# Column maxima of k by 32x32 transposes and a trip through DRAM, and another order of the first loads, in a fused linear-attention and expert kernel

## The chip, the cores and the metric

The kernel runs on one core of a Trainium2 chip. The metric is the device time of one execution in microseconds (us), the median of several runs. Before the change it is 898.88 us, the median of 3 runs (898.53 to 898.95).

## The reference

The first half is linear attention over 8 batches, 8 heads, 576 positions and 64 channels: q is normalised by a softmax over its channels, k by a softmax over its positions, and no score matrix is formed. The second half is a two-layer network over the 4608 tokens with an activation between its layers.

```python
q_s = np.exp(q - np.max(q, axis=-1, keepdims=True))
q_s = q_s / (np.sum(q_s, axis=-1, keepdims=True) + 1e-09)
k_s = np.exp(k - np.max(k, axis=2, keepdims=True))      # over the 576 positions
k_s = k_s / (np.sum(k_s, axis=2, keepdims=True) + 1e-09)
kv = np.einsum('bhsd,bhse->bhde', k_s, v)
x = np.einsum('bhsd,bhde->bhse', q_s, kv)               # tokens x 512
h = x @ w_in                                            # 512 x 2048
g = h * np.clip(h + 3.0, 0.0, 6.0) / 6.0
return (g @ w_out).astype(np.float32)                   # 2048 x 512
```

What the change touches is the maximum of each of k's columns over the 576 positions.

## The kernel before, in words

Two heads are worked on together (a "head pair" `hp`, four of them to a batch, called a head below), so that 2 x 64 channels fill the 128 partitions. Tokens go in nine blocks `j` of 512. The float32 products run as three products of a high and a low part each (`split`, L121). The weights come as float64 pairs of words (`load_w`, L126, 1 MB for each of 16 slices `f`) and are decoded to float32 high and low parts by ScalarE and VectorE (`decode`, L134).

Blocks 0 and 1 use plain products (`gemm1`, L557, and `gemm2`, L574); beside block 1, sums of weights are formed and written to DRAM (`fast_weights`, L446). Blocks 2 to 8 use `fast_pair` (L493): seven smaller products in place of eight for a pair of slices, whose weights are fetched from DRAM by `fetch` (L481) into a ring of twelve places, one new fetch after each product. `fill` (L656) puts the second layer's products of the pair before between them. `steps` (L627) hands out the attention of the next block in small steps, two to a pair.

Attention for one head is `attention` (L305). In batches 0 and 1 ("early") k arrives transposed, channels on partitions; its maxima lie one to a partition, where the exponential can use them as a bias, and TensorE flips the result. From batch 2 on k arrives twice: transposed (`kt`, one buffer) for the maximum alone, and straight (`ke`, two buffers), positions on partitions, in which form it is used. There the maximum is needed as a row, the same on all partitions. VectorE reduces `kt` to `km` (L333); GpSimd spreads it over 128 columns in `kb` (L335, one buffer); TensorE flips `kb` into `pm` in PSUM (L347, through `flip`, L96, so that its trace line is L97); VectorE subtracts `pm` from `ke` (L348) and ScalarE takes the exponential (L351). `kv_of` (L201) then forms the product with v (`pkv`), and `px` (from L374 on) multiplies it with q.

The order of instructions on each engine is fixed when the program is built, by a scheduler that works through a simulated time: whichever instruction is ready first goes first, and among those that are ready the one that stands earlier in the program. From block 1 on TensorE's instructions stay in program order (`ordered`, L85). Nearly all transfers are issued by SP, whose queue is in order too: an issue that waits holds those behind it. At the start ScalarE's queue issues the four loads of q for batch 0 (L193).

The start (L604 to L613): for each of four heads `load_first` issues kT on SP and q on ScalarE's queue; the first half of weight slice 0 goes after head 1; then the four v, the second half of slice 0, and slices 1 to 5.

Of the kernel before, what the change touches and what calls it, by code (L numbers as in the profile page):

```python
# [10 lines left out]
F32 = mybir.dt.float32  # L11
F32R = mybir.dt.float32r
U32 = mybir.dt.uint32
AF = mybir.ActivationFunctionType
# [4 lines left out]
P = 128  # L19
TB = 512  # L20
QD = 32
# [9 lines left out]
def attention_moe(  # L31
# [27 lines left out]
    nc = tc.nc  # L59

    B, NP, _, S = kT.shape
# [6 lines left out]
    NCH = S // P + 1  # L68
# [5 lines left out]
    att = ctx.enter_context(tc.tile_pool(name="att", bufs=1))  # L74
    xp = ctx.enter_context(tc.tile_pool(name="xp", bufs=2))
    moe = ctx.enter_context(tc.tile_pool(name="moe", bufs=2))
    dr = ctx.enter_context(tc.tile_pool(name="dr", bufs=1, space=bass.MemoryType.DRAM))
    ps_a = ctx.enter_context(tc.tile_pool(name="ps_a", bufs=2, space=PSUM))
# [6 lines left out]
    def ordered(ins):  # L85
        if in_order:
            tc.keep_in_program_order(ins)
# [8 lines left out]
    def flip(out, in_):  # L96
        ordered(nc.tensor.transpose(out, in_, ident))  # L97
# [7 lines left out]
    three = const.tile([P, 1], F32, name="three")  # L105
# [5 lines left out]
    def place(f, dt, name):  # L111
        return wp.tile([P, 4 * DM], dt, name=name, tag=f"w{f}")
# [13 lines left out]
    def load_w(f, sides=(0, 1)):  # L126
        if f not in raws:
            raws[f] = place(f, U32, f"raw{f}")
        a, b = 2 * DM * sides[0], 2 * DM * (sides[-1] + 1)
        nc.sync.dma_start(  # L130
            raws[f][:, a:b], w[f].rearrange("p s n -> p (s n)")[:, a:b]
        )
# [56 lines left out]
    def load_first(hp):  # L189
        t = borrow(f"kq{hp}")  # L190
        kt, qt, qT = t[:, 0:S], cut(t, S, NC4, 2, D), t[:, S + TB : S + 2 * TB]
        nc.sync.dma_start(kt, kT[0, hp])
        nc.scalar.dma_start(qt, q[0, hp])  # L193
        t = borrow(f"kv{hp}")
        vt, ke = cut(t, 0, NCH, 2, D + 1), cut(t, NCH * 2 * (D + 1), NCH, P)
        first[hp] = kt, qt, qT, vt, ke

    def load_first_v(hp):
        nc.sync.dma_start(first[hp][3], v[0, hp])
# [60 lines left out]
    def k_softmax(j, km, ke, kt):  # L260

        nc.vector.tensor_reduce(km, kt, axis=AX.X, op=ALU.max, negate=True)
        nc.scalar.activation(kt, kt, AF.Exp, bias=km)
        yield
        pool, tag = (ps_a, "pa") if j else (ps_o, "po")
        pe = pool.tile([P, TB], F32, name="pe", tag=tag)
        pe2 = pool.tile([P, TB], F32, name="pe2", tag=tag)
        for c in range(NC4):
            flip(pe[:, c * P : (c + 1) * P], kt[:, c * P : (c + 1) * P])
        flip(pe2[0:TAIL, 0:P], kt[:, TB:S])  # L270
        nc.scalar.copy(ke[:, 0:NC4].rearrange("p c n -> p (c n)"), pe)
        nc.scalar.copy(ke[0:TAIL, NC4], pe2[0:TAIL, 0:P])
# [32 lines left out]
    def attention(j, hp):  # L305
# [5 lines left out]
        if not j:  # L311
            kt, qt, qT, vt, ke = first[hp]
        else:
            if j < B:
                kt = att.tile([P, S], F32, name="kt", bufs=1)
                nc.sync.dma_start(kt, kT[j, hp])
                ke = att.tile([P, NCH, P], F32, name="ke", bufs=2)
# [9 lines left out]
        if j < B:  # L327
            km = att.tile([P, 1], F32, name="km", bufs=2)
            if early:
                ks = k_softmax(j, km, ke, kt)  # L330
                next(ks)
            else:
                nc.vector.tensor_reduce(km, kt, axis=AX.X, op=ALU.max)  # L333
                kb = att.tile([P, P], F32, name="kb", bufs=1)
                nc.gpsimd.tensor_copy(kb, km.broadcast_to([P, P]))  # L335
        if early:
            q_softmax(qt, j == 1, nc.vector if j else nc.gpsimd)
        else:
# [3 lines left out]
        if early:  # L342
            next(ks, None)
        elif j < B:

            pm = ps_a.tile([P, TB], F32, name="pm", tag="pa")
            flip(pm[:, 0:P], kb)  # L347
            nc.vector.tensor_sub(  # L348
                ke, ke, pm[:, 0:P].rearrange("p (o n) -> p o n", o=1).broadcast_to([P, NCH, P])
            )  # L350
            nc.scalar.activation(ke, ke, AF.Exp)  # L351
        if early:
            pool, tag = (ps_a, "pa") if j else (ps_o, "po")
# [19 lines left out]
        pool, tag = (ps_a, "pa") if j else (ps_h, "ph")  # L373
# [217 lines left out]
    def store(j, po):  # L591
        for t in range(NTT):
# [8 lines left out]
                    nc.scalar.mul(ob, po[t], 1.0 / 6.0)  # L601
            nc.sync.dma_start(out[j * TB + t * P : j * TB + (t + 1) * P, :], ob)

    for hp in range(NP):  # L604
        load_first(hp)
        if hp == 1:
            load_w(0, (0,))
    for hp in range(NP):
        load_first_v(hp)
    load_w(0, (1,))  # L610
    AHEAD = 6
    for f in range(1, AHEAD):
        load_w(f)  # L613
    units = [attention(0, hp) for hp in range(NP)]
    for unit in units:
        next(unit)
# [10 lines left out]
    def steps():  # L627
        for j in range(1, NB):
            heads = range(NP) if j < FAST else (0, 2, 1, 3)
            for hp in heads:  # L630
                unit = attention(j, hp)
                for step in range(4):
                    next(unit, None)
                    if j == FAST and step == 3 and hp != 3:
                        continue
                    yield
                next(unit, None)
# [121 lines left out]
```

## Time and profile before

| what | before |
|---|---|
| median of 3 runs | 898.88 us |
| the profiled execution | 901.36 us |
| its span, first to last instruction | 899.0 us |
| TensorE busy (matmul) | 862.0 us, 96% |
| VectorE busy | 624.6 us, 69% |
| ScalarE busy | 459.1 us, 51% |
| GpSimd busy | 149.0 us, 17% |
| granted TensorE clock, mean | 0.992 |
| moved by DMA | 182.04 MB |

Engines are named PE (TensorE's matmuls), PEld (its weight loads), DVE (VectorE), ACT (ScalarE), POOL (GpSimd) and SP. Matmuls are pipelined, so that the durations of single ones overlap: what one costs is read from the distance between starts. The shares of busy time are means over stretches that differ, so they are read stretch by stretch.

### The profile page before, as it was taken

What the parts mean: (1) busy time and instruction counts of PE and PEld (TensorE: products, weight loads), DVE (VectorE), ACT (ScalarE), POOL (GpSimd) and SP (SyncE); (2) the same over time, 40 slices, a digit from 0 to 9 for tenths busy, and PEclk for the clock granted to TensorE, in tenths of its full rate; (3) what the DMA queues carried; (4) which work ended last, traced back from release to release, by engine and by line L of the source; (5) the groups of instructions that cost most, each with busy time, mean ns of one, the idle gap of its engine ahead of it and who ended that gap; (6) DMA issues with size and microseconds to landing.
All of it is one profiled execution on the core that took longest, in us unless ns stands there. A gap on an engine that the chain in (4) does not pass through costs nothing.

```text
span 899.0 us, 15285 instructions
## 1 busy us (share of the span) xinstructions
PE 862.0 (96%) x5380; PEld 737.0 (82%) x5380; DVE 624.6 (69%) x1265; ACT 459.1 (51%) x937; POOL 149.0 (17%) x329
## 2 busy tenths in 40 slices
PE   5799979999989999999999999999999999999998
PEld 3567656878778888888888888888888888988896
DVE  6999998889767666676776676767676655444333
ACT  6998634445445445545545554445554544443333
POOL 4021432130302121112121211112121200100000
PEclk9999999999999999999999999999999999999999
DMA  9983432538568667766776677776755565557541
GB/s 362 415 330 110 126 105 71 172 106 286 171 210 267 210 213 235 234 213 209 230 239 213 211 223 249 217 216 189 245 170 165 166 220 174 172 174 224 170 141 47
DMA packets 96986, 182.04 MB, mean 202 GB/s; under 512 B 9744, under 2 KB 24080, under 8 KB 94992
## 3 DMA queue, kind: packets, MB, share of 16 engines
q1 hardware_dynamic: 96336, 180.03, 62.0%
q10 hardware_dynamic: 576, 1.05, 0.4%
q8 instruction: 43, 0.70, 0.3%
q14 instruction: 31, 0.25, 0.1%
HBM read 156.93 MB, written 24.12 MB: 201 GB/s over the span
## 4 chain that ended last, share of the span: by engine, by line
PE 72%; DVE 7%; DMA 4%; ACT 2%; issue 1%; POOL 0%; SPq 0%; DVEq 0%; ACTq 0%; POOLq 0%
PE po L91 35%; PE ph L91 28%; PE pz L91 4%; DMA qt<-in_qf_dram 2%; PE pkv L91 2%; PE px L91 2%; DVE qT_lo L124 1%; DMA out_dram<-ob 1%; DVE w L124 1%; DVE m L302 1%; ACT qT_hi L123 1%; DVE x_hi L124 1%; DVE ob L599 1%; DVE x_lo L124 0%; DMA wf<-w 0%
## 5 line engine op out<-in xcount | busy, mean ns | idle before, releaser
L91 PE MATMUL po<-w,w 128*128 128x512 f32 x1008 | 261.5, 394 | 1.3 <-DVE ob L599 0.9
L91 PEld LDWEIGHTS po<-w,w 128*128 128x128 f32 x1008 | 178.4, 189 | 31.9 <-DVE ob L599 2.3
L91 PE MATMUL ph<-x_lo,w 128*128 128x256 f32 (+1 forms) x800 | 152.0, 304 | 1.1 <-ACT second L529 0.8
L91 PEld LDWEIGHTS ph<-w,w 128*128 128x128 f32 x1008 | 133.5, 190 | 13.9 <-DVE second L530 4.9
L91 PE MATMUL ph<-w,w 128*128 128x256 f32 x1008 | 140.6, 284 | 3.0 <-DVE second L530 3.0
L91 PE MATMUL ph<-x_hi,w 128*128 128x256 f32 (+1 forms) x592 | 138.3, 338 | 4.7 <-ACT w L123 3.4
L91 PEld LDWEIGHTS ph<-x_lo,w 128*128 128x128 f32 x800 | 116.6, 189 | 15.8 <-ACT second L529 1.2
L123 ACT CAST w<-g 128x512 fp32r<-128x512 f32 x112 | 69.5, 620 | 86.4 <-DVE g L536 43.5
L91 PEld LDWEIGHTS ph<-x_hi,w 128*128 128x128 f32 x592 | 93.4, 192 | 19.5 <-ACT w L123 5.5
L124 DVE TENSOR_TENSOR w<-g,w 128x512 fp32r<-128x512 f32 x112 | 77.1, 689 | 39.6 <-ACT w L123 39.5
L91 PE MATMUL po<-w 128*128 128x512 f32 x336 | 86.8, 394 | 0.1
L91 PE MATMUL po<-w,g_hi 128*128 128x512 f32 x256 | 70.1, 413 | 3.3 <-ACT g_hi L123 3.3
L124 DVE TENSOR_TENSOR qT_lo<-m,qT_hi 128x512 fp32r<-128x512 f32 x28 | 25.9, 925 | 66.4 <-ACT qT_hi L123 66.3
L91 PEld LDWEIGHTS po<-w 128*128 128x128 f32 x336 | 59.4, 188 | 10.8 <-ACT w L123 0.5
L91 PEld LDWEIGHTS po<-w,g_hi 128*128 128x128 f32 x256 | 48.1, 194 | 15.8 <-ACT g_hi L123 5.5
L284 POOL COPY swap<-qm 32x16 f32<-32x16 f32 x112 | 35.3, 316 | 125.0 <-DVE qm L292 120.9
L551 ACT ACTIVATE g<-second,three 128x512 f32<-128x512 f32 x56 | 40.5, 723 | 29.8 <-DVE second L549 27.3
L535 ACT ACTIVATE g<-ph,three 128x256 f32<-128x256 f32 x56 | 26.5, 473 | 56.0 <-PE ph L91 55.6
L552 DVE SCALAR_TENSOR_TENSOR g<-g,second 128x512 f32<-128x512 f32 x56 | 38.9, 695 | 19.8 <-ACT g L551 19.8
L91 PE MATMUL pz<-x_hi,w 128*128 128x256 f32 x336 | 49.4, 283 | 0.0
L530 DVE TENSOR_TENSOR second<-second,ph 128x256 f32<-128x256 f32 x56 | 23.0, 410 | 36.7 <-ACT second L529 36.6
L536 DVE SCALAR_TENSOR_TENSOR g<-g,ph 128x256 f32<-128x256 f32 x56 | 23.2, 414 | 31.5 <-ACT g L535 31.5
(121 smaller groups left out, 1265.5 us busy)
## 6 DMA issues: line engine op xcount, KB each, us to landing
w<-wf SPq DMA_DIRECT2D x392, 256.0 KB, 3.1
raw<-in_w_dram SPq DMA_DIRECT2D x15, 1024.0 KB, 14.5
out_dram<-ob SPq DMA_DIRECT2D x36, 256.0 KB, 3.2
vt<-in_v_dram SPq DMA_DIRECT2D x28, 325.0 KB, 3.5
wf<-w SPq DMA_DIRECT2D x16, 512.0 KB, 4.2
kt<-in_kT_dram SPq DMA_DIRECT2D x28, 288.0 KB, 2.9
ke<-in_k_dram SPq DMA_DIRECT2D x24, 320.0 KB, 2.9
qt<-in_qf_dram SPq DMA_DIRECT2D x28, 256.0 KB, 3.1
```

The lines of the kernel that those rows point to most:

```text
L91: nc.tensor.matmul(out, lhsT, rhs, start=start, stop=stop, skip_group_check=goes_on)
L123: nc.scalar.copy(hi, src)
L124: engine.tensor_sub(lo, src, hi.bitcast(F32))
L284: nc.gpsimd.tensor_copy(swap[r : r + QD], stat[o : o + QD])
L302: nc.vector.transpose(qT, qt)
L530: nc.vector.tensor_add(second[:, HT:], second[:, HT:], y)
L535: nc.scalar.activation(r[:, HT:], x, AF.Relu, bias=three, scale=1.0)
L536: nc.vector.scalar_tensor_tensor(r[:, HT:], r[:, HT:], 6.0, x, op0=ALU.min, op1=ALU.mult)
L551: nc.scalar.activation(r, second, AF.Relu, bias=three, scale=1.0)
L552: nc.vector.scalar_tensor_tensor(r, r, 6.0, second, op0=ALU.min, op1=ALU.mult)
L599: nc.vector.tensor_scalar_mul(ob, po[t], 1.0 / 6.0)
```

## The change

From batch 2 on the maximum takes another way. GpSimd spreads `km` over 32 columns only (`kx[:, 0]`); VectorE transposes the four 32x32 blocks of it (`kx[:, 1]`), after which the first partition of each block holds 32 maxima as a row; SP stores those four rows (512 bytes in all) to DRAM (`kd`, two buffers) and loads them again into all 128 partitions (`kb`, 64 KB). VectorE subtracts `kb`, which is now in SBUF. TensorE's flip and its place in PSUM go.

At the start, an exponential of one column (`three`) is put ahead of everything, after which `three` is written anew by GpSimd. Slice 0 of the weights is loaded whole after head 1, the v of heads 0 and 1 go behind kT of heads 2 and 3, and the v of heads 2 and 3 follow.

```diff
             else:
                 nc.vector.tensor_reduce(km, kt, axis=AX.X, op=ALU.max)
+                kx = att.tile([P, 2, QD], F32, name="kx", bufs=1)
+                nc.gpsimd.tensor_copy(kx[:, 0], km.broadcast_to([P, QD]))
+                nc.vector.transpose(kx[:, 1], kx[:, 0])
+                kd = dr.tile([P], F32, name="kd", bufs=2)
+                nc.sync.dma_start(kd.rearrange("(r n) -> r n", n=QD), kx[0:P:QD, 1])
                 kb = att.tile([P, P], F32, name="kb", bufs=1)
-                nc.gpsimd.tensor_copy(kb, km.broadcast_to([P, P]))
+                nc.sync.dma_start(
+                    kb, kd.rearrange("(o n) -> o n", o=1).broadcast_to([P, P])
+                )
...
         elif j < B:
-            pm = ps_a.tile([P, TB], F32, name="pm", tag="pa")
-            flip(pm[:, 0:P], kb)
             nc.vector.tensor_sub(
-                ke, ke, pm[:, 0:P].rearrange("p (o n) -> p o n", o=1).broadcast_to([P, NCH, P])
+                ke, ke, kb.rearrange("p (o n) -> p o n", o=1).broadcast_to([P, NCH, P])
             )
             nc.scalar.activation(ke, ke, AF.Exp)
...
+    nc.scalar.activation(three, three, AF.Exp)
+    nc.gpsimd.memset(three, 3.0)
     for hp in range(NP):
         load_first(hp)
         if hp == 1:
-            load_w(0, (0,))
-    for hp in range(NP):
+            load_w(0)
+        if hp > 1:
+            load_first_v(hp - 2)
+    for hp in (2, 3):
         load_first_v(hp)
-    load_w(0, (1,))
```

## Rows read from the trace of the kernel before

**Rows 1.** The profile's page: the busy time of each engine with its share of the span, and what the transfers moved in 40 equal slices of the span.

```profile
PE 862.0 (96%) x5380; PEld 737.0 (82%) x5380; DVE 624.6 (69%) x1265; ACT 459.1 (51%) x937; POOL 149.0 (17%) x329
...
GB/s 362 415 330 110 126 105 71 172 106 286 171 210 267 210 213 235 234 213 209 230 239 213 211 223 249 217 216 189 245 170 165 166 220 174 172 174 224 170 141 47
```

**Rows 2.** Busy time by stretches. Columns: the stretch and its length in us, the busy time of each engine in it with the number of instructions, the granted TensorE clock, the share of the DMA engines' time, GB/s.

```profile
30.00:142.00 112.00, 99.83 (x472) 74.30 (x472) 108.26 (x152) 78.98 (x158) 26.30 (x23) 0.96 0.54 195
142.00:250.00 108.00, 107.17 (x549) 85.47 (x548) 92.44 (x196) 50.55 (x92) 26.15 (x62) 1.00 0.52 168
...
300.00:700.00 400.00, 397.85 (x2728) 351.94 (x2727) 274.74 (x611) 199.02 (x426) 67.46 (x185) 1.00 0.69 216
```

**Rows 3.** The waits of TensorE from 28 to 142 us: what waited for whom, us in all, times, the longest.

```profile
PE px L91 <- DVE kv L213: 7.3, 3, 3.9
```

**Rows 4.** The waits of TensorE from 142 us to the end, the longest group.

```profile
PE ph L91 <- DVE second L530: 3.0, 5, 1.8
```

**Rows 5.** TensorE in order of time from 368 to 390 us: start, us, then engine, line, operation, what it writes and reads, and how many.

```profile
384.40 0.27 PE L97 MATMUL pm<-ident,kb 128*128 128x128 f32 x1
...
385.23 1.75 PE L91 MATMUL po<-w,w 128*128 128x512 f32 x7
386.81 0.88 PE L91 MATMUL ph<-x_lo,w 128*128 128x256 f32 x6
387.53 1.55 PE L91 MATMUL po<-w,w 128*128 128x512 f32 x6
```

**Rows 6.** The waits of VectorE from 4 to 32 us.

```profile
DVE m L146 <- ACT m L145: 2.3, 2, 2.0
DVE qr L255 <- POOL kq L258: 0.8, 1, 0.8
DVE qr L255 <- ACT kq L254: 0.8, 1, 0.8
```

**Rows 7.** SP's queue in order of time from 0 to 9 us: when the two halves of the first weights are issued.

```profile
1.65 0.43 SPq L130 DMA_DIRECT2D raw<-in_w_dram  x1
...
8.45 0.44 SPq L130 DMA_DIRECT2D raw<-in_w_dram  x1
```

**Rows 8.** The transfers issued from 0 to 8 us, and those issued at 8.4 to 8.5 us: times, KB each, us from issue to landing (first half, second half).

```profile
raw<-in_w_dram SPq DMA_DIRECT2D x1, 512.0 KB, 6.4
...
raw<-in_w_dram SPq DMA_DIRECT2D x1, 512.0 KB, 6.6
```

**Rows 9.** ScalarE in order of time from 3 to 17 us. In brackets: how long it was idle before, and what ended that.

```profile
4.53 1.28 ACT L263 ACT_TABLE_LOAD   x1 [4.53 <-DMA kq<-in_kT_dram]
5.82 1.47 ACT L263 ACTIVATE kq<-kq,km 128x576 f32<-128x576 f32 x2
...
16.18 1.15 ACT L145 ACTIVATE m<-raw 128x1024 f32<-128x1024 f32 x1
```

**Rows 10.** All engines in order of time from 0 us: ScalarE's queue issuing the four q loads, and GpSimd writing `three`.

```profile
0.74 1.85 ACTq L193 DMA_DIRECT2D kq<-in_q_dram  x4
...
1.02 0.10 POOL L106 MEMSET three<- 128x1 f32 x1
```

**Rows 11.** Groups of instructions by line and shape, over the whole span: busy us, mean ns of one, then the idle time before them.

```profile
L302 DVE STREAM_TRANSPOSE m<-qt 128x512 f32<-128x512 f32 x28 | 19.6, 700 | 0.0
...
L300 DVE TENSOR_TENSOR qt<-qt,qr 128x512 f32<-128x512 f32 x28 | 19.3, 688 | 0.7
...
L285 DVE TENSOR_TENSOR qm<-qm,swap 128x16 f32<-128x16 f32 x28 | 4.8, 170 | 8.1 <-POOL swap L284 8.1
```

**Rows 12.** The instructions on the tile `pm`: duration in ns (least, median, most), start of the first and of the last in us, shapes.

```profile
L97 PE MATMUL pm<-ident,kb x24: 270/271/272, 158.8 to 687.9; 128*128 128x128 f32 x24
L348 DVE TENSOR_TENSOR ke<-ke,pm x24: 801/809/823, 159.1 to 688.3; 128x640 f32<-128x640 f32 x24
```

**Rows 13.** The same view of the tile `ke`: its loads.

```profile
L319 SPq DMA_DIRECT2D ke<-in_k_dram x24: 328/333/497, 96.0 to 646.6; - x24
```

**Rows 14.** VectorE in order of time from 110.5 to 161.5 us: the maxima of k, the first, third and fourth of 24 (the second lies between the first two).

```profile
110.61 0.75 DVE L333 TENSOR_REDUCE km<-kt 128x1 f32<-128x576 f32 x1
...
121.09 0.74 DVE L333 TENSOR_REDUCE km<-kt 128x1 f32<-128x576 f32 x1
...
160.77 0.74 DVE L333 TENSOR_REDUCE km<-kt 128x1 f32<-128x576 f32 x1
```

**Rows 15.** The view of the tensor `out_dram`: its 36 stores of 256 KB, from issue to landing.

```profile
DMA to landing us min/median/max: 2.0/3.2/4.6
```

**Rows 16.** TensorE in order of time from 368 to 390 us: the first products of two successive pairs.

```profile
367.77 0.88 PE L91 MATMUL pz<-x_hi,w 128*128 128x256 f32 x6
...
378.98 0.87 PE L91 MATMUL pz<-x_hi,w 128*128 128x256 f32 x6
```

**Rows 17.** All engines in order of time from 236 to 264 us: one of VectorE's scalings of the output.

```profile
258.85 0.69 DVE L599 TENSOR_SCALAR ob<-po 128x512 f32<-128x512 f32 x1 [3.74 <-DMA out_dram<-ob]
```

**Rows 18.** The same view: TensorE's two waits around it.

```profile
258.10 0.97 PE L91 MATMUL ph<-x_lo,w 128*128 128x256 f32 x6 [0.83 <-ACT second L529]
...
260.86 0.98 PE L91 MATMUL ph<-w,w 128*128 128x256 f32 x6 [1.79 <-DVE second L530]
```

**Rows 19.** Busy time by stretches again, columns as in rows 2: the granted clock after that wait.

```profile
261.80:265.10 3.30, 3.30 (x16) 3.11 (x15) 3.30 (x8) 1.93 (x4) 0.00 (x0) 0.50 0.61 190
```

**Rows 20.** The waits from 250 us to the end: VectorE for the loads of q.

```profile
DVE qm L292 <- DMA qt<-in_qf_dram: 16.0, 16, 2.2
```

## The prediction, made before the changed kernel was run

> **What bounds the kernel now.** I began with the share of each engine: TensorE is busy for 96% of the span [rows 1], so the time is TensorE's work plus its gaps, and the question is where the gaps lie and who makes them. The table by stretches answers it [rows 2]. From 30 to 142 us VectorE is busy for 108.26 of 112 us and TensorE for only 99.83: VectorE, which still decodes the weights, sets the pace. From 142 to 250 us TensorE is busy for 107.17 of 108, from 300 to 700 us for 397.85 of 400: there the pace is TensorE's, and VectorE (275 of 400) has room. TensorE's waits agree: from 28 to 142 us the longest, 7.3 us, are for VectorE's kv [rows 3]; from 142 us to the end its longest group is 3.0 us [rows 4]. So three rules. An instruction taken from TensorE after 142 us is gained whole. A microsecond that VectorE gains or loses before 142 us moves all that follows by about one. VectorE's work after 142 us is free while it has room.
>
> **Part 1: the flips leave TensorE.** Of 24 heads (batches 2 to 7, four each) one 128x128 transpose goes. Its own duration, 0.27 us, is not its price, since matmuls overlap. From the start of the transpose at 384.40 to the next po group at 385.23 are 0.83 us; the same six products without it take 0.72 us (386.81 to 387.53) [rows 5]. So one costs 0.11 us, and 24 cost 2.6 us, all after 142 us: **-2.6 us**. Bounds: 0, if TensorE then waits where it worked before, and 24 x 0.27 = -6.5. The wait that goes with the flip (for kb) shows on TensorE nowhere in [rows 3, 4], so nothing more is won there.
>
> **Part 2: the order at the start.** VectorE has three stops between its first load and 32 us that another order could fill: 2.3 us for the decode's first operation, 0.8 us for GpSimd's product and 0.8 us for an exponential [rows 6], 3.9 us together. The long one is a load: the second half of the first weights is issued at 8.45 us [rows 7] and needs 6.6 us [rows 8], so it is there at about 15.1, and ScalarE begins to decode at 16.18 [rows 9]. In the new order both halves go as one transfer of 1 MB third in SP's queue; the first half was issued at 1.65 and needed 6.4 us, so it was there at 8.1. The transfers run at 415 GB/s once they are under way (second of the 40 slices [rows 1]), so 512 KB take 1.3 us and the whole is there at about 9.4. What pays is what is moved behind it: head 2's keys come 1.3 us later, head 3's keys 1.3 + 0.8 (behind one v of 325 KB) = 2.1 us later, the v of heads 1 to 3 about 1.3 us later; ScalarE's queue for q shares the same engines and its third and fourth load come about 1.3 us later. While VectorE waits for those, it has the decode's five operations at hand, if the schedule puts it there. I take the two stops of 2.0 and 0.8 us after 12.9 us as filled and give 0.8 back for the later heads: **-2.0 us**, between -3.9 (all stops filled) and +1.9.
>
> The +1.9 comes from the new exponential of one column. Today the table load of 1.28 us starts at 4.53, when the first keys are there, and the first exponential at 5.82 [rows 9]. Hiding it is worth 1.3 us on ScalarE and can shorten only the stop for the exponential, which the 3.9 us hold already; I count it at zero. But the new instruction needs `three`, written at 1.02 to 1.12 us, and ScalarE's queue also issues the four q loads from 0.74 us on [rows 10]. If it stands ahead of them, the first q is issued at 1.12 + 1.28 + 0.2 = 2.6 instead of 0.74 us: 1.9 us late, and q's maxima with it. I think it stands behind at least the first load, as that needs nothing. The memset that restores `three` waits for ScalarE on GpSimd's queue, whose next work, head 0's subtraction, needs q's maxima first: nothing. The Trainium skill (ScalarE: Activation LUTs, What ACT_TABLE_LOAD costs) adds a drain of about 1.4 us to the load's 1.28; by it this step would give up to 2.7 us. The trace disagrees: the exponential begins 1.29 us after the load does, with no drain between them [rows 9].
>
> **Part 3: what VectorE gets.** 24 transposes of 128x32. The nearest rows are 0.70 us for 128x512 and 0.17 us for a 128x16 operation [rows 11]; I take 0.2 us, as at 32 columns the fixed part rules (ends 0.15 and 0.70). The subtraction now reads SBUF twice; 128x512 with both operands there takes 0.69 us [rows 11], so 128x640 takes 0.86 against 0.81 now [rows 12]. After 142 us that is 21 x 0.25 = 5 us in VectorE's idle 31%: zero, and at most 5 us were that room gone. GpSimd's copy becomes smaller, on an engine that waits most of the time: zero.
>
> Before 142 us it counts. Three of the maxima already run there, the first at 110.61 and the last at 121.09 us; the fourth only at 160.77 [rows 14], because kb is held until the first flip, in TensorE's order, at 158.8 [rows 12]. That brake goes. The subtractions no longer wait for TensorE: k has two buffers and is loaded from 96.0 us on [rows 13], while the first subtraction comes at 159.1 [rows 12]. And kx, kd and kb together can hold more maxima. So work from after 142 us, where it was free, can be pulled to where VectorE is full. The least is three transposes, 0.6 us; the most two subtractions (1.6), three more maxima (2.2) and their transposes (1.0), 4.8 us. The other way, the three maxima could fall behind 142 us: -2.2. I take the three transposes and one subtraction: **+1.4 us**.
>
> **Part 4: the trip through DRAM.** Per head SP gets a store of 512 bytes, which waits for the transpose, and a load of 64 KB, which waits for the store and for the subtraction of the head before. Landing takes 2.0 us in the quickest store of the trace and 3.2 in the middle [rows 15], so the trip takes 4 to 6.4 us. Between two heads lie (687.9 - 158.8) / 23 = 23.0 us [rows 12]: it is covered, **0 us**. Behind these two on SP stand the weight loads, the stores and the loads of q, k and v. The weights come twelve products ahead, at seven products in 11.2 us (from one pz group to the next [rows 16]), that is 19 us less 2 to 5 for landing: SP may stand for some 14 us before TensorE starves. The bytes are 1.6 MB more on 182. The Trainium skill speaks against such a step (DMA: Bandwidth & Descriptors, Anatomy of one DMA): about 2.0 us per transfer whatever its size, so about 4 us for the pair, which for 24 heads would add 96 us if nothing lay beside it. The rows agree on the 2 us and show the cover of 23.
>
> **Sum.** -2.6 - 2.0 + 1.4 + 0 = -3.2 us. The profiled execution took 901.36 us (span 899.0), so it would take 898.2; its distance to the median of the runs, 898.88, is 2.5 us, which I keep: **895.7 us**, 0.35% faster.
>
> **Rivals.** *The start gives nothing back.* The later heads, or q behind the table load, hold VectorE as long as the decode did (part 2 between -1 and +1.9), or more maxima are pulled forward. For it: attention's last head, not the decode, ended the wait before the first products (TensorE's longest wait there is for VectorE's kv [rows 3]). Against it: 2 us of that stop are plainly the load's. With part 2 at zero and part 3 at +2.2: 898.5 us. That is also the time if the steps do nothing that counts, the flip's 2.6 us apart.
>
> *Slower: VectorE stuck behind a transfer at a pair's sixth or seventh product.* VectorE works in order; its subtraction now waits for a transfer (kb, or k itself, which so far had landed long before the flip), and SP's longer queue delays stores and q loads. The price is seen once: at 258.85 us VectorE had waited 3.74 us for a store of the output, TensorE then 0.83 and 1.79 us [rows 17, 18], and its granted clock fell to 0.50 (1.2 GHz) from 261.8 to 265.1 us [rows 19], 1.7 us more: 4.3 us. Against it: 16 waits for q, 16.0 us together [rows 20], cost TensorE almost nothing, so a wait decides only from about 3.5 us on. Two more such places give -3.2 + 8.6: 904.3 us.
>
> *Faster than the sum:* the stop at 258.85 goes, because four subtractions have left the stretch before it: -3.2 - 4.3, 891.4 us.
>
> **Chances.** Forecast 0.50, nothing from the start 0.20, slower 0.18, faster than the sum 0.12. A change of 0.2%, 1.8 us, is about what can be told from none here. Of the forecast's cases 0.06 fall within it, with part 3 near its upper end; of the first rival 0.16 do, and 0.02 on either side; of the slower one 0.02, a single short stop. So faster 0.44 + 0.02 + 0.12 = 0.58, same 0.24, slower 0.02 + 0.16 = 0.18. For 8 in 10 the range runs from 891.5 (all stops at the start filled and nothing pulled forward give 892.4, and the fastest case lies below) to 900.5 (the start lost at +1.9 and 2.3 pulled forward); beyond it lie the slower rival's price and half of the fastest.
>
> **What would show it.** Right: no pm rows; a po group 0.71 us after a six-product group at each of those places; the first decode near 10 us and no stop of 2 us on VectorE between 13 and 18; the table load over before 4.5 us; L333 and the subtraction waiting for no transfer. Wrong: q loads issued after 2.5 us; five or more maxima, or subtractions, before 142 us with TensorE's waits there above the present ones; VectorE's subtraction behind a transfer for over 3.5 us with a wait of TensorE right after it.

## The result and the profile after

The changed kernel took 908.37 us (median of 4 runs, 906.72 to 910.28) against 898.91 for the kernel before (898.53 to 899.58): ratio 1.0095, 95% interval 1.0078 to 1.0112. It is slower by about 9.5 us, where 895.7 was forecast. The profiled execution took 910.28 us, span 908.3, 9 us more than the one before (901.36, 899.0).

TensorE's busy time moved by 1.2 us [rows 1], so 8 of the 9 us are gaps:

```profile
PE 863.2 (95%) x5356; PEld 738.8 (81%) x5356; DVE 631.3 (70%) x1289; ACT 455.9 (50%) x938; POOL 149.7 (16%) x330
```

To find the gaps I divided both traces at the same places in the work: at block 1's first product, at the first product of the first `fast_pair` (block 2), and at the last product. The table by stretches, columns as in [rows 2], first of before, then of after:

```profile
0.00:149.84 149.84, 122.80 (x628) 90.99 (x629) 136.89 (x205) 103.60 (x194) 39.86 (x46) 0.97 0.60 224
149.84:249.97 100.13, 99.30 (x514) 79.11 (x513) 85.20 (x187) 48.22 (x88) 21.91 (x57) 1.00 0.54 175
249.97:894.90 644.93, 639.53 (x4240) 566.88 (x4238) 401.88 (x874) 306.97 (x655) 87.19 (x226) 1.00 0.65 201
```

```profile
0.00:143.60 143.60, 120.83 (x628) 91.24 (x629) 136.91 (x204) 104.85 (x197) 40.79 (x49) 0.95 0.63 235
143.60:260.90 117.30, 104.64 (x509) 82.11 (x508) 101.32 (x232) 46.77 (x87) 27.21 (x73) 0.96 0.59 191
260.90:903.84 642.94, 637.28 (x4220) 565.47 (x4219) 392.35 (x854) 303.95 (x654) 81.66 (x208) 1.00 0.63 197
```

Up to block 1 after is 6.2 us ahead, blocks 2 to 8 give 2.0 more, and block 1 alone loses 17.2: 100.1 us became 117.3, with 16 us more of VectorE in it. What VectorE does there that it did later before, or not at all, in after and then in before (groups by line and shape, columns as in [rows 11]):

```profile
L333 DVE TENSOR_REDUCE km<-kt 128x1 f32<-128x576 f32 x20 | 14.8, 739 | 2.4 <-DMA kt<-in_kT_dram 2.2
...
L337 DVE STREAM_TRANSPOSE kx<-kx 128x32 f32<-128x32 f32 x21 | 4.2, 202 | 2.0 <-POOL kx L336 1.7
```

```profile
L333 DVE TENSOR_REDUCE km<-kt 128x1 f32<-128x576 f32 x5 | 3.7, 742 | 0.0
```

The tiles of after say how far these ran ahead (columns as in [rows 12 to 14]):

```profile
L333 DVE TENSOR_REDUCE km<-kt x24: 702/742/754, 124.7 to 238.5; 128x1 f32<-128x576 f32 x24
...
L339 SPq DMA_DIRECT2D kd<-kx x24: 499/500/1139, 127.0 to 245.2; - x24
L341 SPq DMA_DIRECT2D kb<-kd x24: 319/320/955, 128.6 to 636.9; - x24
L354 DVE TENSOR_TENSOR ke<-ke,kb x24: 805/824/827, 133.4 to 659.5; 128x640 f32<-128x640 f32 x24
```

All 24 maxima, transposes and stores lie between 124.7 and 245.2 us; the loads of `kb` and the subtractions that use them come as late as 636.9 and 659.5. Before, the maxima were spread out as the subtractions were: eight of them by the first fast pair, where after has all 24. The two buffers of `kd` held nothing: the stores were up to 16 heads ahead of the loads. If `kd` has only two places in DRAM, most of these rows were overwritten before they were loaded. Whether they were is not shown, and the result hardly tells: a softmax over the positions does not depend on what was subtracted from its column, but for overflow and the 1e-09.

How TensorE felt it, its waits in block 1 in after and then in before:

```profile
PE px L91 <- DVE kv_lo L124: 4.8, 4, 1.5
PE px L91 <- ACT kv_hi L123: 4.6, 3, 2.3
PE po L91 <- ACT g_hi L123: 2.4, 2, 2.0
PE po L91 <- DVE g_lo L124: 0.8, 1, 0.8
```

```profile
PE po L91 <- ACT g_hi L123: 0.6, 1, 0.6
PE po L91 <- DVE g_lo L124: 0.2, 1, 0.2
```

12.6 us of waits against 0.8. The other 5.3 us are in TensorE's busy time (104.64 against 99.30) and are mostly clock: in after three stretches of 3.4 us at 0.50 (1.2 GHz) stand in block 1, in before none. That is about half their length, 1.7 us for each, and each begins at most 1.0 us after one of these waits ended (product started at 148.54 after 1.97 us, at 193.40 after 1.51, at 237.30 after 2.32):

```profile
149.50:152.90 3.40, 2.84 (x7) 2.29 (x8) 3.33 (x9) 1.14 (x2) 1.11 (x4) 0.50 0.31 91
193.90:197.30 3.40, 3.40 (x9) 2.67 (x8) 3.40 (x5) 2.93 (x7) 2.70 (x3) 0.50 0.16 33
238.30:241.70 3.40, 3.11 (x8) 2.55 (x9) 2.06 (x5) 2.88 (x7) 1.72 (x3) 0.50 0.99 359
```

So block 1 is 99.3 us of products, plus waits, plus clock; the same sum, with 98 to 100 us of products, holds for every kernel below.

One head (the third of block 1) shows how a wait arises: VectorE in after, in order of time, from the first `rk` to `kv_lo`, then ScalarE, then TensorE:

```profile
209.06 0.14 DVE L210 TENSOR_SCALAR rk<-pkv 128x1 f32<-128x1 f32 x1
209.13 0.73 DVE L333 TENSOR_REDUCE km<-kt 128x1 f32<-128x576 f32 x1
...
210.63 0.83 DVE L354 TENSOR_TENSOR ke<-ke,kb 128x640 f32<-128x640 f32 x1
211.37 0.15 DVE L211 RECIPROCAL rk<-rk 128x1 f32<-128x1 f32 x1
...
212.37 0.34 DVE L213 SCALAR_TENSOR_TENSOR kv<-pkv,rk,mask 128x128 f32<-128x128 f32 x1
...
215.99 0.21 DVE L337 STREAM_TRANSPOSE kx<-kx 128x32 f32<-128x32 f32 x1
216.13 0.25 DVE L124 TENSOR_TENSOR kv_lo<-kv,kv_hi 128x128 fp32r<-128x128 f32 x1
```

```profile
213.28 0.69 ACT L573 ACTIVATE g<-ph,three 128x512 f32<-128x512 f32 x1 [1.00 <-PE ph L91]
213.87 0.61 ACT L123 CAST w<-ob 128x512 fp32r<-128x512 f32 x1
214.38 0.30 ACT L123 CAST kv_hi<-kv 128x128 fp32r<-128x128 f32 x1
```

```profile
206.47 0.95 PE L91 MATMUL pkv<-vt,ke 128*64 128x65 f32 x20
...
214.73 0.44 PE L91 MATMUL px<-qT_hi,kv_hi 128*128 128x384 f32 x1 [1.26 <-ACT kv_hi L123]
...
216.43 0.45 PE L91 MATMUL px<-qT_hi,kv_lo 128*128 128x384 f32 x1 [1.09 <-DVE kv_lo L124]
```

From `pkv` a chain goes over `rk`, `kv`, the cast `kv_hi` on ScalarE and `kv_lo` back to TensorE's `px`, which has a fixed place in TensorE's order, 6.6 us behind `pkv`. A maximum of a much later head and a subtraction of a later one stand inside the chain, a transpose stands ahead of `kv_lo`, and VectorE and ScalarE both work in order. ScalarE has its share: `kv` is done at 212.71 us, but `kv_hi` begins at 214.38, behind `g` and a cast of `w`. In the same head before, `px` started at 208.67 us, 6.6 us after its `pkv` at 202.12, with no wait.

The other heads agree. From the end of `pkv` to the product of `px` that needs `kv_lo`, each of the four heads of block 1 takes 6.3 us in before and 8.5 to 9.7 in after, 11.2 us more together. In the chains (from `pkv` to `kv`, and from `kv_hi` to `kv_lo`) VectorE does in after 3.9 us of maxima, 1.3 of their transposes and 3.3 of subtractions from `ke`, and in before none of the three. The subtractions can stand there because no flip ties them to TensorE's order any more.

The start went as argued, and further. VectorE's waits from 4 to 32 us [rows 6] are gone but for the last, and ScalarE [rows 9, 10] has its table early and decodes at 8.84 us in place of 16.18:

```profile
DVE km L262 <- DMA kq<-in_kT_dram: 4.2, 1, 4.2
DVE qr L255 <- ACT kq L254: 0.8, 1, 0.8
```

```profile
0.74 0.41 ACTq L193 DMA_DIRECT2D kq<-in_q_dram  x1
1.18 1.28 ACT L611 ACT_TABLE_LOAD   x1 [1.18 <-PEq L751]
1.24 1.35 ACTq L193 DMA_DIRECT2D kq<-in_q_dram  x3
...
8.84 1.13 ACT L145 ACTIVATE m<-raw 128x1024 f32<-128x1024 f32 x1
```

(VectorE's first wait here is for the first keys; before it was 4.5 us.)

### The profile page after: what moved, and what is told of

Read it like the earlier page. It is cut to its first block, busy times and chain, and to the rows that moved or that the text cites. A ratio compares the mean times of both kernels' runs of the same rounds, so it can differ in the third digit from the quotient of the medians.

```text
span 908.3 us, 15294 instructions
## 1 busy us (share of the span) xinstructions
PE 863.2 (95%) x5356; PEld 738.8 (81%) x5356; DVE 631.3 (70%) x1289; ACT 455.9 (50%) x938; POOL 149.7 (16%) x330
## 4 chain that ended last, share of the span: by engine, by line
PE 70%; DVE 12%; DMA 5%; issue 2%; ACT 2%; POOL 0%; SPq 0%; DVEq 0%; POOLq 0%; ACTq 0%
PE po L91 34%; PE ph L91 27%; PE pz L91 4%; PE px L91 2%; PE pkv L91 2%; DMA qt<-in_qf_dram 2%; DMA kt<-in_kT_dram 1%; DVE qT_lo L124 1%; DVE km L333 1%; DVE g L574 1%; DVE v L157 1%; DVE m L302 1%; DVE x_hi L124 1%; DVE g_lo L124 1%; DVE x_lo L124 1%
## 5 line engine op out<-in xcount | busy, mean ns | idle before, releaser
L91 PE MATMUL ph<-x_lo,w 128*128 128x256 f32 (+1 forms) x800 | 150.1, 302 | 2.0 <-ACT second L535 1.7
L91 PE MATMUL po<-w,g_hi 128*128 128x512 f32 x256 | 72.6, 424 | 3.8 <-ACT g_hi L123 3.8
L91 PEld LDWEIGHTS po<-w,g_hi 128*128 128x128 f32 x256 | 50.4, 202 | 16.7 <-ACT g_hi L123 5.4
L536 DVE TENSOR_TENSOR second<-second,ph 128x256 f32<-128x256 f32 x56 | 23.1, 412 | 40.3 <-ACT second L535 40.0
```

The costliest lines, as they stand in the source:

```text
L91: nc.tensor.matmul(out, lhsT, rhs, start=start, stop=stop, skip_group_check=goes_on)
L536: nc.vector.tensor_add(second[:, HT:], second[:, HT:], y)
```

## The experiments

Theory: the maxima run ahead because nothing holds them any more, and in block 1 they stand ahead of the chain that TensorE waits for. Rivals: the trip itself (a wait for a transfer, or SP's queue); the new start; and, later, VectorE's busy time as such. "Stretches" below are, in this order: to block 1's first product, block 1, from the first fast pair to the last product (before: 149.8, 100.1, 644.9). Ratios are to the kernel before on the same chip, with 95% intervals. A stretch is that of the one profiled execution, which lies 4.3 us below the median in experiment 2, 7.2 above it for the table load in 5 (its stretches are not used), and within 2.6 elsewhere.

**1. The new start alone** (the kernel before with the last part of the diff).

> The kernel before with the new start alone (the exponential of three, the first loads in the new order); the maxima keep their flips. Theory A (run-ahead): the loss sits in block 1, because the new path no longer holds the maxima back and about 15 more of them are done on VectorE there. It expects the start's gain undisturbed: the last decode near 135 us, block 1 (its first product to the first pz) about 100 us long as before, 892 to 894 us in all. Theory B (the trip's waits: SP, GpSimd and VectorE held by transfers): the same, 892 to 894. Theory C (the new start itself brings the schedule of block 1 into disorder): block 1 longer by over 10 us, 905 or more.

Measured 899.0 us, 0.9979 (0.9962 to 0.9996); stretches 142.8, 105.3, 645.2. Block 1 begins 7 us sooner, but takes 5.2 us longer (4.4 of waits, one slow stretch of the clock), so that the 892 to 894 us of theories A and B are missed. The start is worth 0.2%, and is not where the loss is.

**2. The new path alone** (the changed kernel with the old start).

> The kernel before with the new path of the maxima alone; the loads at the start as before. Theory A: block 1 about 17 us longer, the rest 2 us shorter: 911 to 916 us. Theory B: the same. Theory C: without the new start no disorder, 896 to 897 us.

Measured 920.92, 1.0220 (1.0189 to 1.0251); stretches 156.5, 111.6, 642.2. The loss is in this part, more than expected, and the start hides some of it. Only 11.5 us of it lie in block 1, and 6.6 ahead: ten maxima now lie before block 1, where VectorE sets the pace, in place of three.

**3. Running ahead without any trip.**

```diff
-            km = att.tile([P, 1], F32, name="km", bufs=2)
+            km = att.tile([P, 1], F32, name="km", bufs=26)
```

> The kernel before with one number changed: km has 26 buffers in place of 2, so that VectorE may reduce the maxima of all heads early. No trip through DRAM, flips as before, loads as before; VectorE's work is the same in amount. Theory A: maxima move into block 1 (about 20 there in place of 5, 11 us of VectorE), TensorE waits at px there, 906 to 912 us. Theory B: no transfer was added, so 899 us within 2. Theory C: 899 within 2.

Measured 912.05, 1.0129 (1.0104 to 1.0153); stretches 154.0, 110.2, 642.4. Flips, `kb` in one buffer and loads are those of before; only `km` lets the maxima go. They do (14 of the 24 in block 1 and ten ahead of it), and it costs 1.3%, where the new path with the same start costs 2.2 (experiment 2). The maxima, block 1's row and TensorE's longest waits in it:

```profile
L333 DVE TENSOR_REDUCE km<-kt x24: 735/744/754, 113.0 to 220.1; 128x1 f32<-128x576 f32 x24
```

```profile
154.04:264.23 110.19, 102.88 (x515) 81.41 (x513) 92.70 (x197) 47.20 (x88) 20.18 (x57) 0.97 0.59 184
```

```profile
PE px L91 <- DVE kv_lo L124: 5.5, 2, 3.1
PE px L91 <- ACT kv_hi L123: 0.9, 1, 0.9
```

**4. The change with the maxima held:** `kx` and `kb` as one tile of one buffer, so that the next head's copy waits for this head's subtraction.

```diff
-                kx = att.tile([P, 2, QD], F32, name="kx", bufs=1)
+                kxb = att.tile([P, 2 * QD + P], F32, name="kxb", bufs=1)
+                kx = kxb[:, 0 : 2 * QD].rearrange("p (a n) -> p a n", a=2)
...
-                kb = att.tile([P, P], F32, name="kb", bufs=1)
+                kb = kxb[:, 2 * QD :]
```

> The changed kernel with kx and kb in one tile of one buffer, so that a head's maxima can be spread only after the subtraction of the head before: the trip through DRAM stays, the run-ahead goes. Theory A: about 5 maxima in block 1, block 1 about 100 us, 889 to 893 us. Theory B: the trip and its waits are all there, 904 to 909 us. Theory C: 904 to 909 us.

Measured 901.58, 1.0017 (0.9998 to 1.0037); stretches 143.6, 104.4, 646.9. The trip, the transposes and the subtraction from SBUF are all there, and 0.78 of the 0.95% are gone. The maxima and block 1's row:

```profile
L333 DVE TENSOR_REDUCE km<-kt x24: 703/709/747, 125.0 to 582.4; 128x1 f32<-128x576 f32 x24
```

```profile
143.61:247.98 104.37, 99.46 (x509) 78.59 (x508) 88.80 (x197) 47.23 (x87) 21.45 (x57) 1.00 0.53 173
```

So it is not the trip: block 1 takes 104.4 us, as with the start alone (105.3), in place of 117.3. The total lies between what the theories gave (889 to 893, and 904 to 909). What remains against the start alone (899.0) is in the last stretch: VectorE waits 15 times, 23.1 us, for `ke` itself (nothing in before), and a stretch of slow clock at 257.2 us lasts 6.8 us in place of 3.4.

**5. Single parts of the change.** The table load (the first two new lines of the start, alone):

> The kernel before with the exponential of three at the head alone; loads as before. If the start's gain (block 1 begins 7 us earlier with the whole new start) is the loads', this is 0 to -1 us against the kernel before, block 1 beginning at 149 to 150 us. If it is the table load's, block 1 begins near 143 us and the kernel takes 2 us less.

900.38, 0.9998 (0.9976 to 1.0020): nothing. The loads' order alone:

> The kernel before with the new order of the first loads alone. If the gain is the loads': block 1 begins at 142 to 145 us, block 1 takes about 105 us, and the whole is 1.5 to 2 us less than before, as with the whole new start. If it is the table load's: no change, block 1 from 149 us.

898.5, 0.9974 (0.9955 to 0.9992): the whole of the start. The flip left out and nothing else (VectorE subtracts `kb` as GpSimd wrote it):

> The kernel before with the flip left out and no trip: the subtraction reads kb from SBUF as GpSimd wrote it, so the maxima subtracted are not those of the columns. It asks why blocks 2 to 8 did not get the flips' 2.1 us (19 x 0.11) in the held kernel. Theory D (the trip's transfers cost them): without the trip blocks 2 to 8 take 642 to 643.5 us against 644.9. Theory E (the subtraction, no longer tied to TensorE's order, waits on VectorE for its load of k, and the flips' price is hidden or given back there): 644.5 to 647 us, with VectorE's waits for k's load near 20 us as in the changed kernel. In both, theory A expects two subtractions and one or two maxima more before the first pz, which comes 2 to 5 us later than before, so the whole is 899 to 904 us.

903.23, 1.0024 (1.0008 to 1.0041), a loss: TensorE's share fell as it should (638.8 us busy in the last stretch, 3.4 of it lost to the clock, against 639.5 with 1.7 lost: 2.4 less), but without the flip the subtraction waits for `ke` as in 4, and the slow stretch of the clock at 262.4 us is 6.8 us long in place of 3.4. The stretch takes 644.9 us with the flips and without them.

**6. A tighter brake:** `km` with one buffer, with the new start, with the held change (4), with the loads' order, and alone; and with six buffers.

```diff
-            km = att.tile([P, 1], F32, name="km", bufs=2)
+            km = att.tile([P, 1], F32, name="km", bufs=1)
```

> The kernel before with the new start, and km with one buffer in place of two: one maximum fewer can run ahead. Theory A: VectorE's work before the first pz falls by one or two maxima (0.7 to 1.5 us), block 1 is 1 to 2 us shorter than the 105.3 of the new start alone, the whole 0.5 to 2 us less than it. If run-ahead does not matter at this size, the same time as the new start alone.

> The changed kernel with kx and kb in one tile of one buffer and km with one buffer: the trip through DRAM with the least run-ahead. Theory A: 8 maxima before the first pz (the kernel as changed has 24), first pz at 245 to 248 us; blocks 2 to 8 take 645 to 647 us as in the held kernel with two km, since what the flips give there is lost again to waits: 0.995 to 0.999 of the kernel before. If the trip itself costs, above the kernel before.

> The kernel before with the new order of the first loads and one km buffer, with flips and without the exponential of three. Theory A, with the table load worth nothing: the same as the new start with one km buffer, 0.994 of the kernel before within 0.003.

> The kernel before with one km buffer in place of two, start and flips as before. It tells how much of the 0.6% that the new start with one km buffer won is km's. Theory A: one maximum fewer before the first pz and its place in VectorE's order after the decodes; 0.5 to 2 us less, 0.998 to 0.9995 of the kernel before.

> The kernel before with six km buffers in place of two: four more maxima (12 in place of 8) before the first pz, 3.0 us more of VectorE there. Theory A expects a loss in proportion: with 16 more the first pz came 14.3 us later, so 3 to 5 us later here and 1.003 to 1.006 of the kernel before. If only some threshold (VectorE full) counts, no loss within 0.2%.

| kernel | us | ratio | stretches |
|---|---|---|---|
| start, `km` 1 | 895.11 | 0.9942 (0.9917 to 0.9967) | 141.4, 104.9, 643.6 |
| held change, `km` 1 | 896.01 | 0.9947 (0.9928 to 0.9966) | 140.0, 105.0, 643.0 |
| loads' order, `km` 1 | 893.42 | 0.9924 (0.9901 to 0.9947) | 140.3, 102.2, 644.7 |
| before, `km` 1 | 901.36 | 0.9997 (0.9982 to 1.0011) | 148.4, 104.6, 643.9 |
| before, `km` 6 | 901.56 | 1.0013 (0.9996 to 1.0030) | 150.8, 102.3, 644.3 |

With the brake the loads' order earns 0.8% in place of 0.3% and the whole start 0.6 in place of 0.2, more than expected, and the held change is no better than the flips that it replaces (0.9947 against 0.9942 with the same start). Alone the brake does nothing, and four more maxima ahead of block 1 (seven in place of three) cost 0.13%, 0.3 at most, less than expected: the loss is not so much per maximum.

**7. VectorE's time as such.** Sixteen, then eight reductions of 0.68 us whose result nobody reads, in block 1 behind each slice's work:

```diff
             fill()
+            if j == 1:
+                none = att.tile([P, 1], F32, name="none", bufs=2)
+                nc.vector.tensor_reduce(none, g[0].bitcast(F32), axis=AX.X, op=ALU.max)
             pend.append(work(j, [f], [g]))
```

> The kernel before with 16 idle reductions on VectorE in block 1, one for each weight slice: the maximum of g_hi (128x512, about 0.68 us each, 10.9 us in all) into a tile that nobody reads. No transfer, no maximum moved, nothing else changed. Theory A in its strict form (block 1 goes at VectorE's pace, each microsecond there costs about one): block 1 takes 108 to 112 us in place of 100.1, the whole 907 to 912 against a kernel before of about 901. Theory F (the loads of kT that come along with the early maxima, or their place before block 1, do the harm, not VectorE's time in block 1): 901 to 903.

> The same with 8 idle reductions, in every second slice of block 1, 5.4 us of VectorE. Theory A strict: 905 to 907 against about 901. Theory A with room (some idle time of VectorE in block 1 takes the first few microseconds, the loss begins above it): 901 to 903. Theory F: 901 to 902.

898.11, 0.9966 (0.9951 to 0.9982) and 898.33, 0.9968 (0.9948 to 0.9988): *faster* than before, with 11 and 5 us more of VectorE in block 1. Neither theory has that. Block 1 was 3.6 and 5.3 us longer, but the last stretch 8.5 us shorter. Busy time as such does not account for the loss; the gain needed an explanation of its own, which is the next run: the same tile, and no reductions.

```diff
+            if j == 1 and not f:
+                none = att.tile([P, 1], F32, name="none", bufs=2)
+                nc.gpsimd.memset(none, 0.0)
```

> The kernel before with the small tile `none` of the two kernels with idle reductions, two buffers of 4 bytes a partition, written once by GpSimd and read by nobody: the same tiles in SBUF as there, and none of the reductions. There the stretch from the first fast pair to the end was 8.5 us shorter (636.4 against 644.9 us), with the same products and the distance between successive first products 113 ns in place of 119, second-layer products 228 in place of 232. If it is where the tiles stand in SBUF: the same distances here, 636 to 637 us in that stretch, and block 1 shorter than the kernel before's 100.1 by 0 to 1.5 us; ratio 0.989 to 0.992. Then the idle reductions cost block 1 what lies between this block 1 and theirs (4 to 5 us). Rival, it was the reductions or another order that they brought: distances and stretch as in the kernel before, ratio 0.999 to 1.001.

894.88, 0.9941 (0.9922 to 0.9959). The three stretches, columns as above:

```profile
0.00:150.10 150.10, 124.08 (x628) 91.62 (x629) 136.85 (x205) 103.28 (x194) 39.71 (x47) 0.95 0.60 224
150.10:250.82 100.72, 99.56 (x514) 78.90 (x513) 85.29 (x187) 48.29 (x88) 21.93 (x57) 1.00 0.54 174
250.82:888.10 637.28, 632.52 (x4239) 562.62 (x4238) 401.06 (x874) 306.69 (x655) 87.51 (x226) 1.00 0.66 204
```

Each engine has the same work as before, to an instruction or two, and TensorE needs 7.0 us less for it in the last stretch (5.3 without the slow stretch at 261.7 us that before has there): the gain comes with the tile, not with the reductions. (The median is a little above what was expected.) Against this block 1 of 100.7 us, 11 us of idle reductions cost 3.0 us, although VectorE had only 15 us of 100 free; they show as waits of `px` for `kv_hi` and `kv_lo` (3.1 us), so some of them fell into the chain too. (The eight cost 4.7, more than the sixteen: a wait of 2.6 us for an exponential of `ke` and a slow stretch of the clock fell into that block.)

**8. The same time inside the chain.**

```diff
-        nc.vector.scalar_tensor_tensor(
+        for _ in range(8 if j == 2 else 1):
+            nc.vector.scalar_tensor_tensor(
```

> The kernel before, with the operation that forms kv (0.34 us) done eight times in place of once for the four heads whose px stands in block 1, each time with the same result: 4 x 7 x 0.34 = 9.6 us more of VectorE there, about as much as 16 idle reductions (11 us), but all of it in the chain from pkv over kv, kv_hi and kv_lo to px. No tile is added. Theory: what counts is what stands ahead of that chain in VectorE's order, as TensorE waits at px; in the kernel before px comes some 0.5 us after kv_hi is there, so four waits of about 1.9 us, 7 to 8 us, and up to two slow stretches of the clock (1.7 us each): block 1 107 to 111 us with waits of px for kv_hi and kv_lo, ratio 1.007 to 1.012. Rival, the rule of the prediction, that VectorE's work after 142 us is free while VectorE has room: block 1 100 us, ratio 0.999 to 1.001.

917.62, 1.0195 (1.0171 to 1.0218). Block 1's row, its added operations (five of the 33 were there), and TensorE's longest waits in it:

```profile
149.79:269.25 119.46, 106.65 (x514) 83.39 (x513) 97.26 (x217) 48.50 (x88) 20.50 (x57) 0.94 0.44 147
```

```profile
L214 DVE SCALAR_TENSOR_TENSOR kv<-pkv,rk,mask 128x128 f32<-128x128 f32 x33 | 11.3, 343 | 0.6
```

```profile
PE px L91 <- ACT kv_hi L123: 10.0, 4, 4.1
PE pkv L91 <- ACT ke L352: 2.0, 1, 2.0
```

Four waits for the four heads, as in after; 12.6 us of waits and about 7 of clock. Block 1 grew by 19.3 us, twice the 9.6 us put in and more than expected, while the other two stretches stayed (149.8 and 644.3). So 11 us of VectorE spread over the block cost 3 us, and 9.6 us in the chain cost 19.

**9. The best version:** the loads' order, `km` with one buffer, and the idle tile with two or three buffers.

> The loads' order and one buffer of `km`, as in the best kernel so far (0.9924), with the tile `none` of two buffers: one small buffer fewer in all than in the kernel with idle reductions. If the place in SBUF sets the distances of products, this is a third place, and its stretch from the first fast pair to the end lies anywhere from 636 to 645 us, ratio 0.983 to 0.993. Without such an effect 0.992 to 0.993.

> The same with three buffers of `none`, so that all that stands behind both tiles stands where it stood with the idle reductions. If the place sets the distances: 113 and 228 ns, 636 to 637 us from the first fast pair on, about 8 us less than that kernel's 893.4 us: 885, ratio 0.982 to 0.985. Without such an effect 0.992 to 0.993.

893.36, 0.9929 (0.9909 to 0.9949), and **887.85, 0.9866 (0.9842 to 0.9890)**; last stretches 643.3 and 637.8. Only the second, in which the tiles behind `km` and `none` stand where they stood in 7, has the short products. It falls a little short of the 885 us expected. It is 13.2 us faster than the kernel before on its chip (901.05), and 2.3% faster than the changed kernel (0.9866 / 1.0095).

## Why the prediction was wrong, point by point

**The step that failed is part 3,** and with it the third rule of the first part. I saw that the brake on the maxima goes (`kb` held until a flip in TensorE's order), and then took +1.4 us for it and bounded it by three more maxima and two subtractions (+4.8), because only VectorE's stretch before 142 us seemed to count. Block 1 alone took 17.2 us more, of which 5.2 come with the new start alone. In fact nothing in the new path holds a maximum except the store of `kd` that frees `kx` (31.9 us in ten waits of GpSimd): all 24 ran, and 20 of them beside block 1. Ahead of block 1 the bound held: one more maximum, three transposes and two subtractions. But "VectorE's work after 142 us is free while it has room" is false for block 1. The room is an average: experiment 8 lost 19.3 us in a block in which VectorE was busy for 85 of 100 us. Between `pkv` and `px` VectorE has little room, since `px` has its place in TensorE's order: in the kernel before two of the four heads had `kv_lo` ready 0.1 and 0.4 us before it was needed, the other two 2.4 and 2.7. The trace held this: block 1's chain could have been read off for one head, and the question "what stands there if maxima of later heads are ready" asked.

That the loss is the run-ahead is shown from both sides: it comes without the trip (experiment 3: +10.1 us in block 1, +4.2 ahead of it) and goes with the trip in place (experiment 4). What experiment 2 loses beyond 3 (0.9%) comes with the transposes, the untied subtractions or the transfers, which were not separated while the maxima ran ahead. That the price of work on VectorE is set by its place in the order, not by its time, is shown by 7 and 8 with idle work. That each single wait in after was made by the maximum, transpose or subtraction seen in its chain was read off the order, not tried one by one; other operations, ScalarE's among them, came later there too.

**Part 1** had TensorE's work right, and not what it is worth. The last stretch of after has 19 flips fewer and TensorE is busy 2.25 us less in it (637.28 against 639.53), 0.12 us each, with one slow stretch of the clock in either; experiment 2 against 3, both with run-ahead, gives 1.4. But the time did not follow. The last stretch of experiment 2 (no flips) and of 3 (with them):

```profile
268.06:910.26 642.20, 637.35 (x4221) 565.28 (x4219) 393.36 (x857) 304.30 (x655) 81.61 (x208) 1.00 0.63 197
```

```profile
264.23:906.58 642.35, 638.74 (x4240) 566.91 (x4238) 392.94 (x857) 308.23 (x655) 87.51 (x226) 1.00 0.63 195
```

So the 2.0 us that blocks 2 to 8 give in after come with the maxima that left them (experiment 3, which keeps the flips, gives 2.6), and of the -2.6 nothing is seen: its upper bound, 0, came, and "an instruction taken from TensorE after 142 us is gained whole" fails. What I put at nothing was the flip's other role: it held the subtraction back until `ke` had landed. Without it VectorE waits for `ke` in all kernels without flips (16 times, 20.7 us, in after), which I had named as a risk; in experiment 4 and with the flip left out (5) it goes with 1.7 us more of slow clock near 260 us.

**Part 2** had the direction, and a size too small: -2.0 forecast, -3.9 the bound, and -6.2 measured up to block 1. VectorE's stops before block 1 fell by 6.3 us (149.84 - 136.89 to 143.60 - 136.91). I counted the stops up to 32 us alone. But most of it does not reach the end: with the start alone block 1 gives 5.2 of 7.1 us back, and the end comes 1.5 us sooner (899.0 against 900.51). So the second rule, that a microsecond before 142 us moves all that follows by about one, fails too. The table load at zero was right (0.9998), and so was its place: the first q is issued at 0.74 us, ahead of it. The Trainium skill (ScalarE: Activation LUTs, What ACT_TABLE_LOAD costs) puts a switch of tables at about 2.7 us with its drain; the run shows no gain from hiding it.

**Part 4** was right: VectorE waited 0.3 us for `kb` in all and at most 1.9 us at a time for `ke`, and the held change, which keeps the trip, is level with the flips (0.9947 against 0.9942 with the same start). The section of the Trainium skill that the prediction names here (DMA: Bandwidth & Descriptors, Anatomy of one DMA) is on transfers that GpSimd issues; these are issued by SP, and the quickest store took the same 2.0 us [rows 15].

**The rivals.** "Slower" came true in sign only: its mechanism, VectorE stuck behind a transfer, did not happen. Its chance of 0.18 was given to the wrong story. The sign named for "wrong", five or more maxima before 142 us with TensorE's waits there above those before, was not met: four maxima lay there, and TensorE's waits from 28 to 142 us fell from 15.9 to 9.4 us. I had not thought of them behind 142 us at all.

**Open.** Block 1 takes 102 to 105 us in every kernel here that begins it before 144 us with the maxima held. In the best (102.2) TensorE waits 2.4 us there, 2.0 of them for `x_hi` and `x_lo` and none for `px`. An early start is not all of it, as the kernel before with one `km` buffer begins block 1 at 148.4 us and takes 104.6. The cause stays open.

## What to carry to other kernels

A buffer, or a wait on a slow engine, may be what holds early work back; whoever removes it must ask how far that work can run, and which buffer stops it next, and bound the cost by that number, not by the few instances seen near the bottleneck. An engine's idle share says little about a chain that crosses it twice: find the chain whose end has a fixed place in the bottleneck's order, and look at what may be scheduled into it. And before a small difference is put down to an edit, add a control that keeps its tiles and drops its work.

## What the hardware showed that was not expected

The place of tiles in SBUF seems to change how close products follow each other. (The place is inferred, as the traces hold no addresses; the figures are measured.) With a tile of 4 bytes a partition more (two buffers), the mean distance between starts of neighbouring products, waits left out (those over 40 ns above the median), fell from 119.0 to 114.0 ns for the products of `x_hi` into `ph` (256 columns), from 119.0 to 117.6 for those of `x_lo` into `ph`, from 118.4 to 117.1 for `pz`, and from 231.4 to 229.6 for the second layer's (512 columns), while the last group of the first layer (`w` by `w`) stayed at 118.8 to 119.0. Over the last stretch TensorE's busy time fell from 639.5 to 632.5 us, of which 1.7 is one slow stretch of the clock that was gone. Kernels with the same tiles share these figures whatever else differs (three with this place at 636.4 to 637.3 us, and the best version at 637.8); `km` with one buffer has its own, 121.0 for `x_lo` and 229.7 to 229.8 for the second layer's. Which tile's address it is, and what about it matters, stays open.

A transpose of 128x32 takes 0.20 us on VectorE (0.2 was assumed), and the trip's store costs SP 0.50 us to issue, where the load takes 0.32.
